# First weights' sums stored unsplit and split where they are used; their making cut into shorter stages; conversion jobs started less densely

## The chip, the cores and the metric

One core of a Trainium2 chip runs the whole program. The metric is the device time of one execution in microseconds (us), lower is better. The engines are TensorE (PE; its weight loads are listed apart as PEld), VectorE (DVE), ScalarE (ACT), GpSimd (POOL), and SyncE (SP), which issues the DMA transfers here. Each engine works through its own instructions in program order and waits for others by semaphores.

## What is computed

Three parts follow each other, in fp32:

```
ret  = (q k^T / 8 * D_h) v                 per batch element b (8) and head h (8), 576 positions
x    = ret, heads side by side             8 x 576 x 512, here 9 blocks of 512 rows
u    = x + (x^T U V)^T                     rank 32 over the positions
x2   = u + max(u w_ch1, 0) w_ch2           512 -> 2048 -> 512
xk, xr = x2 mixed with the row before it   by mu_k, mu_r
out  = sigmoid(xr w_r) * (max(xk w_k, 0)^2 w_v)
```

D_h is a decaying lower triangle. The weights arrive as 64-bit floats.

## The kernel before, in words

All large products run as three fp32r products each: an operand x is kept as a rounded part h (an ACT copy) and a rest l = x - h (a subtraction on DVE or POOL), and h·h, l·h and h·l are added in PSUM.

**The first stage** (about 0 to 496 us) goes through 40 steps, five per batch element. A step does a piece of the retention on PE (`up`, `dn`, with results taken out by DVE as `pm`, `y`, `w`, `xt`), turns an older piece round (`xn`, copied out by ACT as `xs`), and then runs some products of the first weights, `hidden(t, f)`, for an older block t and one of the 16 groups f of 128 columns of w_ch1: 12 matmuls into one of two PSUM banks, left by an ACT ReLU (`hs`, L389) and a store. When a batch element is complete, its eight rank-32 corrections (`mx`, L1028) are placed between the matmuls of `hidden`. They share one PSUM bank with `xn`: the first `mx` waits until ACT has copied `xs`, and each later one waits until DVE has added the one before into `xt` (L1032).

**Conversion jobs** fill the same stage. A job takes 64-bit weights from DRAM to split fp32r values: load, `down` (ACT reads the raw words, L100 and L104), `fill` (DVE joins them, L107), sums (POOL) where the product needs them, `parts` (ACT copies, POOL subtractions) and stores. There are 10 such jobs (`block_weight`) for w_k, w_r and half of w_ch2, and 8 shorter ones for w_v. A list `waiting` holds them. `slot()` takes each job in flight one stage on; whether it also starts a new one is its argument. It is called twice a step while no corrections are due ("quiet" slots, counted in `quiet`).

**Sums of the first weights.** Blocks 7 and 8, the pair, are done in a stage of their own (496 to about 576 us): by Strassen's scheme seven products, m = 1, 7, 5, 2, 6, 4, 3, replace eight, in each of eight groups g (`first_group`, seven times 6 matmuls). This needs four sums of quarters of w_ch1 for each g. `first_sums(g)` makes them in the first stage, one stage of it in each quiet slot: `whole` (4 DVE additions h + l, L298), `sums` (4 DVE operations, L306 to L309), then for each half `part` (ACT copy L314, DVE subtraction L315) and `store` (512 KB). The last store of one g and the `whole` of the next are one stage. `load_first(g)` reads both halves, 1 MB, one group before they are used.

**The way into the pair's stage.** `operands` makes the seven combinations of the pair's rows from `even` (tiles `ue`) and `odd` (a view of the tile `xt` of the last batch element), in small steps set between the last six `hidden` products. `mix_store` has just issued the stores of that `xt` to DRAM (L1055, L1056).

**In the pair's stage** ACT and DVE also take out the products (`f`), and four more conversion jobs (`second_weight`) run at `tick()`.

Of the kernel before, what the change touches and what calls it, by code (L numbers as in the profile page):

```python
# [9 lines left out]
F32 = mybir.dt.float32  # L10
# [33 lines left out]
def retention_mixer_kernel(ctx: ExitStack, tc: tile.TileContext, io):  # L44
# [242 lines left out]
    kept_1 = [dram.tile([128, 2, 2, 2, 256], F32, name=f"first{g}") for g in range(HF)]  # L287

    def first_sums(g):
        got = {}  # L290

        def whole():
            got["x"] = [cv.tile([128, 512], F32, tag="cf", name="cf", bufs=5) for _ in range(2)]
            for i, x in enumerate(got["x"]):
                f = g + HF * i
                w, c = w1[f // 4], slice((f % 4) * 128, (f % 4 + 1) * 128)
                for k in range(2):
                    nc.vector.tensor_tensor(  # L298
                        x[:, 256 * k:256 * k + 256].rearrange("p (k n) -> p k n", n=128),
                        w.h[k][:, :, c].bitcast(F32), w.l[k][:, :, c].bitcast(F32), op=ALU.add,  # L300
                    )

        def sums():
            x, y = got["x"]
            a11, a12, a21, a22 = x[:, :256], x[:, 256:], y[:, :256], y[:, 256:]
            nc.vector.tensor_tensor(a22, a21, a22, op=ALU.add)  # L306
            nc.vector.tensor_tensor(a21, a11, a21, op=ALU.subtract)
            nc.vector.tensor_tensor(a11, a22, a11, op=ALU.subtract)
            nc.vector.tensor_tensor(a12, a12, a11, op=ALU.subtract)  # L309
# [7 lines left out]
        def store(i):  # L317
            nc.sync.dma_start(
                kept_1[g][:, i], got[i].bitcast(F32).rearrange("p l (s n) -> p l s n", n=256)
            )  # L320

        return [whole, sums, lambda: part(0), lambda: store(0), lambda: part(1), lambda: store(1)]

    fs = {}

    def load_first(g):
        for i in range(2):
            x = fs[g, i] = (big2 if g else big).tile([128, 2, 2, 256], F32R, tag="unit", name=f"fw{g}_{i}")
            nc.sync.dma_start(x.bitcast(F32), kept_1[g][:, i])
# [366 lines left out]
    def operands(x, q, a, b, nm, where=None):  # L696
# [18 lines left out]
        less(b[0], b[0], a[0])  # L715
        yield
        lower()
        lower = upper("t1", b[0])
        yield
        less(t, b[1], b[0])  # L720
# [49 lines left out]
    with ExitStack() as st:  # L770
# [412 lines left out]
        for at, job in zip((0, 2, 4, 6, 8, 10, 12, 14, 16, 17), jobs):  # L1183
            waiting.insert(at, job)
# [58 lines left out]

        def step_of(i):
# [31 lines left out]
            for x in range(2):  # L1276
# [24 lines left out]
        while ready:  # L1301
            if len(ready) == 3:
                load_first(0)
# [25 lines left out]
    def first_group(g, base, extra):  # L1329
# [7 lines left out]
        def summed(lo, part, x, i):  # L1337
            return fs[g, part][:, lo, x, col(i)]
# [9 lines left out]
        for m, (b, new, w, nm) in {  # L1348
            1: ("a", True, lambda lo, i: weight(lo, 0, 0, i), "11"),
            7: ("c", True, lambda lo, i: summed(lo, 0, 0, i), "t3"),  # L1350
            5: ("d", True, lambda lo, i: summed(lo, 0, 1, i), "t1"),
# [346 lines left out]
```

## Time and profile before

| | before |
|---|---|
| three runs, median (lowest to highest) | 1390.14 us (1388.85 to 1391.22) |
| the profiled execution: time, span of its instructions | 1390.9 us, 1389.0 us |
| mean granted clock of TensorE | 0.977 |
| PE busy / DVE / ACT / POOL | 97% / 66% / 49% / 27% |
| DMA queue q1 | 343.06 MB, 69.7% of 16 engines |

The profiled execution lies 0.8 us above the median, so what is worked out on it carries over. PE's 97% includes time at half clock: the granted clock is shown as a share of 2.4 GHz, and 0.50 is 1.2 GHz. Rows of a stretch below read: start:end, length, busy us (and number of instructions) of PE, PEld, DVE, ACT, POOL, then the mean granted clock, the mean busy share of the DMA engines, and GB/s. A wait `X <- Y` means that engine X stood idle until Y had finished; its three numbers are us in total, times, and the longest.

### The profile page before, as it was taken

What the parts mean: (1) busy time and instruction counts of PE and PEld (TensorE: products, weight loads), DVE (VectorE), ACT (ScalarE), POOL (GpSimd) and SP (SyncE); (2) the same over time, 40 slices, a digit from 0 to 9 for tenths busy, and PEclk for the clock granted to TensorE, in tenths of its full rate; (3) what the DMA queues carried; (4) which work ended last, traced back from release to release, by engine and by line L of the source; (5) the groups of instructions that cost most, each with busy time, mean ns of one, the idle gap of its engine ahead of it and who ended that gap; (6) DMA issues with size and microseconds to landing.
All of it is one profiled execution on the core that took longest, in us unless ns stands there. A gap on an engine that the chain in (4) does not pass through costs nothing.

```text
span 1389.0 us, 26137 instructions
## 1 busy us (share of the span) xinstructions
PE 1340.4 (97%) x10248; PEld 1099.0 (79%) x10248; DVE 920.1 (66%) x1268; ACT 677.8 (49%) x1185; POOL 380.9 (27%) x317
## 2 busy tenths in 40 slices
PE   6899898999899999999999999999999999999998
PEld 4688787778687787788888888888888888888897
DVE  3634555546353335769888898698687787787753
ACT  4663444446452356644354444465465455465431
POOL 2440344335370013112122222203303303303312
PEclk8899999999999999999999999999999999999999
DMA  9577789989896277999879696888066075074272
GB/s 356 201 246 240 251 312 348 330 314 347 320 346 235 103 241 277 333 409 359 282 243 319 218 309 211 282 285 328 1 244 240 1 275 210 27 277 152 96 279 81
DMA packets 137547, 344.74 MB, mean 248 GB/s; under 512 B 16592, under 2 KB 32336, under 8 KB 137424
## 3 DMA queue, kind: packets, MB, share of 16 engines
q1 hardware_dynamic: 137424, 343.06, 69.7%
q8 instruction: 81, 1.33, 0.4%
q14 instruction: 42, 0.34, 0.1%
HBM read 235.01 MB, written 108.00 MB: 247 GB/s over the span
## 4 chain that ended last, share of the span: by engine, by line
PE 84%; DMA 7%; DVE 5%; ACT 2%; issue 1%; POOL 1%; SPq 0%; DVEq 0%; ACTq 0%; POOLq 0%
PE h L383 19%; PE v L1543 14%; PE gc L557 6%; PE ga L557 6%; PE gd L557 6%; PE kc L1447 4%; PE kd L1447 4%; PE ka L1447 4%; PE gb L557 3%; PE kb L1447 2%; PE rd L1447 2%; PE rc L1447 2%; PE ra L1447 2%; PE xn L977 1%; PE fa L1360 1%
## 5 line engine op out<-in xcount | busy, mean ns | idle before, releaser
L389 ACT ACTIVATE hs<-h 128x512 f32<-128x512 f32 x112 | 66.7, 597 | 177.1 <-PE h L383 173.2
L1499 POOL TENSOR_TENSOR vl<-m,vh 128x512 fp32r<-128x512 f32 (+1 forms) x40 | 47.6, 1191 | 310.2 <-ACT vh L1498 238.9
L516 ACT CAST sbh<-rb 128x1024 fp32r<-128x1024 f32 x64 | 67.3, 1052 | 49.3 <-PE gd L557 41.0
L1543 PE MATMUL v<-vh,wv_0u 128*128 128x512 f32 x288 | 88.8, 389 | 0.0
L1543 PE MATMUL v<-vh,wv_1u 128*128 128x512 f32 x288 | 88.7, 389 | 0.0
L517 DVE TENSOR_TENSOR sbl<-rb,sbh 128x1024 fp32r<-128x1024 f32 x64 | 84.3, 1317 | 3.4 <-ACT sbh L516 3.3
L516 ACT CAST sah<-ra 128x1024 fp32r<-128x1024 f32 (+1 forms) x64 | 53.5, 836 | 57.7 <-DVE ra L498 28.1
L517 DVE TENSOR_TENSOR sal<-ra,sah 128x1024 fp32r<-128x1024 f32 (+1 forms) x64 | 66.5, 1038 | 18.6 <-PE gd L557 10.4
L1032 DVE TENSOR_TENSOR xt<-mx,xt 128x256 f32<-128x256 f32 x64 | 28.8, 457 | 62.1 <-PE mx L1028 62.1
L1499 POOL TENSOR_TENSOR vl<-c,vh 128x512 fp32r<-128x512 f32 (+1 forms) x40 | 62.1, 1573 | 25.9 <-ACT vh L1498 25.9
L1543 PEld LDWEIGHTS v<-vh,wv_1u 128*128 128x128 f32 x288 | 54.1, 188 | 11.2
L1543 PEld LDWEIGHTS v<-vh,wv_0u 128*128 128x128 f32 x288 | 53.9, 188 | 11.1
L801 POOL TENSOR_TENSOR kv<-kv,ktab 128x512 f32<-128x512 f32 (+1 forms) x40 | 40.8, 1019 | 71.6 <-DMA kv<-in_kv 52.9
L1498 ACT CAST vh<-m 128x512 fp32r<-128x512 f32 (+1 forms) x40 | 23.2, 579 | 75.3 <-DVE m L1497 75.3
L315 DVE TENSOR_TENSOR fs<-cf,fs 128x512 fp32r<-128x512 f32 x16 | 13.8, 865 | 67.2 <-ACT fs L314 67.2
L853 DVE TENSOR_TENSOR pm<-up,dtab 128x512 f32<-128x512 f32 (+1 forms) x40 | 25.3, 632 | 48.7 <-PE up L839 48.6
L1543 PE MATMUL v<-vl,wv_0u 128*128 128x512 f32 x144 | 56.0, 389 | 0.0
L1543 PE MATMUL v<-vl,wv_1u 128*128 128x512 f32 x144 | 56.0, 389 | 0.0
L601 POOL TENSOR_TENSOR x<-x,ur 128x512 f32<-128x512 f32 x16 | 25.0, 1574 | 107.5 <-DVE x L597 101.7
L670 ACT ACTIVATE tp<-x2l,omu 128x511 f32<-128x511 f32 x72 | 50.9, 713 | 2.8 <-issue 2.3
L574 POOL TENSOR_TENSOR m<-m,ur 128x512 f32<-128x512 f32 x8 | 12.2, 1550 | 137.2 <-ACT m L571 137.2
L1497 DVE SCALAR_TENSOR_TENSOR m<-m 128x512 f32<-128x512 f32 (+1 forms) x40 | 44.8, 1119 | 1.4
(377 smaller groups left out, 3982.1 us busy)
## 6 DMA issues: line engine op xcount, KB each, us to landing
wk<-keys SPq DMA_DIRECT2D x80, 512.0 KB, 6.0
rb<-hp SPq DMA_DIRECT2D x64, 512.0 KB, 6.4
hp<-hs SPq DMA_DIRECT2D x112, 256.0 KB, 3.9
wr<-gates SPq DMA_DIRECT2D x40, 512.0 KB, 6.7
qk<-in_qk SPq DMA_DIRECT2D x32, 512.0 KB, 6.8
kv<-in_kv SPq DMA_DIRECT2D x32, 512.0 KB, 6.9
ra<-hp SPq DMA_DIRECT2D x32, 512.0 KB, 7.1
ur<-ub SPq DMA_DIRECT2D x18, 512.0 KB, 6.4
```

The source lines that it names most:

```text
L383: nc.tensor.matmul(hps[t, f], w.part(lo, k, fo), u[k // 2][:, k % 2, :], start=(part == 0 and k == 0), stop=(part == 2 and k == KD - 1),)
L389: nc.scalar.activation(h, hps.pop((t, f)), AF.Relu)
L516: nc.scalar.copy(hi_, src)
L517: nc.vector.tensor_tensor(lo_, src, hi_.bitcast(F32), op=ALU.subtract)
L557: nc.tensor.matmul(group[g][p], l[:, col(p)], r, start=(h == 0 and j == 0 and i == 0), stop=(i == 2 and last), skip_group_check=True,)
L670: nc.scalar.activation(tp[:, 1:], x[:, :BT - 1], AF.Copy, scale=omu[:, j, k:k + 1])
L801: nc.gpsimd.tensor_tensor(k, k, ktab[:, p, :n].to_broadcast([128, n, NP, D]), op=ALU.mult)
L1032: nc.vector.tensor_tensor(u, ps[:, :n], u, op=ALU.add)
L1447: nc.tensor.matmul(ps[b], l, r[:, i], start=(part == 0 and i == 0 and j == 0), stop=(i == 1 and j == 2), skip_group_check=True,)
L1497: nc.vector.scalar_tensor_tensor(x, x, 0.0, x, op0=ALU.max, op1=ALU.mult)
L1499: eng.tensor_tensor(l, x, h.bitcast(F32), op=ALU.subtract)
L1543: nc.tensor.matmul(vacc[t][o], w.part(lo, g, col(o)), x[:, i, :], start=(g == 0 and i == 0 and j == 0), stop=(g == NG - 1 and i == 1 and j ...
```

## The change

First weights' sums: `first_sums` now uses one tile of the pool `big` per g instead of two of the small pool `cf`, has five stages (`whole(0)`, `whole(1)`, `sums(0)`, `sums(1)`, `store`) with two DVE operations in each of the first four, makes no split, and stores 512 KB instead of 1 MB. `load_first` reads 512 KB, two groups ahead; `split_first` does one ACT copy and one DVE subtraction of 128x1024 per g, after m = 2 of the group before. `operands` writes one difference over `a[0]` where it wrote over `b[0]`. Conversion jobs start in three of eight quiet slots instead of four, in another order (three jobs of w_k first), and slots go on into the tail of the first stage (`beside`); the last job ends beside `hidden(6, 4)` where it ended beside `hidden(5, 9)`. First sums begin eight slots later.

```diff
-    kept_1 = [dram.tile([128, 2, 2, 2, 256], F32, name=f"first{g}") for g in range(HF)]
+    kept_1 = [dram.tile([128, 4, 256], F32, name=f"first{g}") for g in range(HF)]
...
-        def part(i):
-            x = got["x"][1 - i]
-            y = got[i] = unit(big, F32R, f"fs{g}_{i}")
-            nc.scalar.copy(y[:, 0], x)
-            nc.vector.tensor_tensor(y[:, 1], x, y[:, 0].bitcast(F32), op=ALU.subtract)
...
-        return [whole, sums, lambda: part(0), lambda: store(0), lambda: part(1), lambda: store(1)]
+        def whole(i):
+            if not i:
+                got["x"] = big.tile([128, 4, 256], F32, tag="unit", name=f"fs{g}")
...
+        def store():
+            nc.sync.dma_start(kept_1[g], got["x"])
+
+        return [lambda: whole(0), lambda: whole(1), lambda: sums(0), lambda: sums(1), store]
...
+    def split_first(g):
+        x = fraw.pop(g)
+        fs[g] = h, l = tuple(
+            (big2 if g else big).tile([128, 4, 256], F32R, tag="unit", name=f"f{y}{g}") for y in "hl"
+        )
+        nc.scalar.copy(h, x)
+        nc.vector.tensor_tensor(l, x, h.bitcast(F32), op=ALU.subtract)
...
-        less(b[0], b[0], a[0])
+        less(a[0], b[0], a[0])
         yield
         lower()
-        lower = upper("t1", b[0])
+        lower = upper("t1", a[0])
...
-        for at, job in zip((0, 2, 4, 6, 8, 10, 12, 14, 16, 17), jobs):
+        for at, job in zip((0, 1, 2, 4, 5, 6, 8, 10, 12, 14), jobs):
...
+        def beside():
+            quiet.append(0)
+            slot(new=len(quiet) % 8 in (1, 4, 6))
+            if sums and len(quiet) > 8:
+                sums.pop(0)()
...
-                    quiet.append(i)
-                    slot(new=len(quiet) % 2 == 1 or len(quiet) > 40)
-                    if sums:
-                        sums.pop(0)()
+                    beside()
...
-            hidden(2)
+            hidden(1)
+            beside()
+            hidden(1)
+            beside()
         while todo:
             hidden(1) if ready else mixes(1)
+            beside()
...
-            if len(ready) == 3:
-                load_first(0)
+            if len(ready) in (4, 3):
+                load_first(4 - len(ready))
+            if len(ready) == 1:
+                split_first(0)
...
-            extra[1] = [lambda g=g: load_first(g + 1)]
+            extra[2] = [lambda g=g: split_first(g + 1)]
+        if g + 2 < HF:
+            extra[4] = [lambda g=g: load_first(g + 2)]
```

On DVE, ahead of the first correction (`mx3_0_0`) of block 3: L107 rows are `fill`s of conversion jobs, L298 to L310 make sums of first weights, L853 to L967 are the retention's, L1032 adds the correction. Before:

```order
L107 SCALAR_TENSOR_TENSOR wkf3_3113<-ca_3117,wkf3_3113 128x512
L107 SCALAR_TENSOR_TENSOR cf_3269<-ca_3268,cf_3269 128x512
L306 TENSOR_TENSOR cf_3274<-cf_3274 128x256
L307 TENSOR_TENSOR cf_3274<-cf_3273,cf_3274 128x256
L308 TENSOR_TENSOR cf_3273<-cf_3274,cf_3273 128x256
L309 TENSOR_TENSOR cf_3273<-cf_3273 128x256
L853 TENSOR_TENSOR pm23_3384<-up22_3318,dtab_126 128x512
L950 TENSOR_TENSOR y22_3386<-up22_3318,qtab_127 128x512
L938 TENSOR_TENSOR w4_6_3388<-dn22_3335,w4_5_3202 128x256
L938 TENSOR_TENSOR w4_7_3390<-dn22_3335,w4_6_3388 128x256
L967 TENSOR_TENSOR xt4_3034<-dn22_3335,y22_3386 128x4x128
L1032 TENSOR_TENSOR xt3_2184<-mx3_0_0_3409,xt3_2184 128x256
```

Of the change:

```order
L107 SCALAR_TENSOR_TENSOR wkf3_3050<-ca_3054,wkf3_3050 128x512
L309 TENSOR_TENSOR fs1_2922<-fs1_2922 128x256
L310 TENSOR_TENSOR fs1_2922<-fs1_2922 128x256
L107 SCALAR_TENSOR_TENSOR wrf0_3224<-ca_3225,wrf0_3224 128x512
L298 TENSOR_TENSOR fs2_3261<-w1_0h0_527,w1_0l0_528 128x256
L298 TENSOR_TENSOR fs2_3261<-w1_0h2_626,w1_0l2_627 128x256
L853 TENSOR_TENSOR pm23_3335<-up22_3269,dtab_126 128x512
L950 TENSOR_TENSOR y22_3337<-up22_3269,qtab_127 128x512
L938 TENSOR_TENSOR w4_6_3339<-dn22_3286,w4_5_3164 128x256
L938 TENSOR_TENSOR w4_7_3341<-dn22_3286,w4_6_3339 128x256
L967 TENSOR_TENSOR xt4_2996<-dn22_3286,y22_3337 128x4x128
L1032 TENSOR_TENSOR xt3_2168<-mx3_0_0_3360,xt3_2168 128x256
```

Between two `fill`s and the retention's rows stood a run of four sum operations, and in the slot before it four more (the next L298 rows upwards); now two and two stand there, and the tile they write is one of `big`.

On ACT, from the take-out of `hidden(4, 11)` (`hs4_11`) to the copy `xs6_1`, for which the first correction of block 5 waits (`wsh`, `wv_0p` casts are splits of conversion jobs, L100 and L104 a job's `down`). Before:

```order
L389 ACTIVATE hs4_11_5002<-h4_11_4989 128x512
L270 CAST wsh5_0_5005<-wsf5_4661 128x512 x2
L100 ACTIVATE ca_5012<-wsraw6_0_4835 128x512
L104 ACTIVATE wsf6_5011<-wsraw6_0_4835 128x512
L100 ACTIVATE ca_5015<-wsraw6_1_4837 128x512
L104 ACTIVATE wsf6_5011<-wsraw6_1_4837 128x512
L314 CAST fs6_1_5022<-cf_4671 128x512
L987 COPY xs6_1_5114<-xn6_1_5109 128x512
```

Of the change:

```order
L389 ACTIVATE hs4_11_4907<-h4_11_4894 128x512
L132 CAST wv_0p3_4716<-cf_4593 128x512
L100 ACTIVATE ca_4917<-wsraw6_0_4742 128x512
L104 ACTIVATE wsf6_4916<-wsraw6_0_4742 128x512
L100 ACTIVATE ca_4920<-wsraw6_1_4744 128x512
L104 ACTIVATE wsf6_4916<-wsraw6_1_4744 128x512
L987 COPY xs6_1_5014<-xn6_1_5009 128x512
```

The split of a first weights' sum (`fs6_1`, L314) is gone, and of the jobs' casts one stands there instead of a pair; the `down` has kept its place.

On DVE, the first rows of `operands` (L706 are differences, L703 subtractions that make the l parts). Before:

```order
L706 TENSOR_TENSOR ft_0_6334<-xt7_5591 128x1024
L703 TENSOR_TENSOR fl11_0_6332<-ue0_6040,fh11_0_6331 128x1024
L706 TENSOR_TENSOR xt7_5591<-xt7_5591,ue0_6040 128x2x512
L703 TENSOR_TENSOR flt3_0_6343<-ft_0_6334,fht3_0_6342 128x1024
L706 TENSOR_TENSOR ft_0_6334<-xt7_5591 128x1024
L703 TENSOR_TENSOR flt1_0_6359<-xt7_5591,fht1_0_6358 128x1024
```

Of the change:

```order
L706 TENSOR_TENSOR ft_0_6270<-xt7_5483 128x1024
L703 TENSOR_TENSOR fl11_0_6268<-ue0_5939,fh11_0_6267 128x1024
L706 TENSOR_TENSOR ue0_5939<-xt7_5483,ue0_5939 128x1024
L703 TENSOR_TENSOR flt3_0_6279<-ft_0_6270,fht3_0_6278 128x1024
L706 TENSOR_TENSOR ft_0_6270<-xt7_5483,ue0_5939 128x1024
L703 TENSOR_TENSOR flt1_0_6295<-ue0_5939,fht1_0_6294 128x1024
```

The third row reads the same two tiles and now writes `ue0`, which was read from DRAM, and no longer `xt7`, which is being stored to DRAM; the rows after it read `ue0`.

## Rows read from the trace of the kernel before

**Rows 1.** PE's waits, 110 to 600 us (total us, times, longest us).

```profile
PE mx L1028 <- DVE xt L1032: 10.6, 4, 4.1
PE h L383 <- ACT hs L389: 5.5, 2, 3.4
PE mx L1028 <- ACT xs L987: 4.8, 2, 2.9
```

**Rows 2.** Nine stretches, A to I, each around one stall of PE.

```profile
161.00:174.00 13.00, 9.36 (x62) 7.03 (x55) 4.98 (x10) 3.34 (x7) 1.85 (x2) 0.74 0.60 204
229.00:239.00 10.00, 5.89 (x18) 4.54 (x17) 5.98 (x11) 0.60 (x1) 4.39 (x6) 0.66 1.03 383
273.00:284.00 11.00, 8.90 (x140) 6.83 (x142) 4.97 (x10) 6.72 (x13) 4.15 (x4) 0.84 1.02 395
297.00:308.00 11.00, 7.95 (x30) 6.08 (x29) 6.49 (x13) 0.99 (x3) 2.09 (x3) 0.84 0.92 334
360.00:372.00 12.00, 7.42 (x23) 5.39 (x23) 4.98 (x10) 3.46 (x6) 1.12 (x2) 0.72 1.03 375
418.00:422.00 4.00, 2.41 (x93) 1.99 (x85) 2.64 (x5) 0.00 (x0) 0.26 (x1) 1.00 1.03 320
481.00:492.00 11.00, 7.58 (x23) 5.72 (x22) 9.75 (x9) 6.61 (x8) 0.00 (x0) 0.69 0.26 74
550.00:553.00 3.00, 1.31 (x6) 0.81 (x5) 0.50 (x1) 1.68 (x3) 0.34 (x1) 1.00 0.90 356
579.00:588.00 9.00, 6.92 (x22) 4.64 (x21) 8.56 (x12) 6.96 (x8) 0.00 (x0) 0.81 0.96 325
```

**Rows 3.** DVE's longest wait, 110 to 485 us.

```profile
DVE fs L315 <- ACT fs L314: 67.2, 15, 10.9
```

**Rows 4.** ACT's wait for raw weights, 110 to 485 us.

```profile
ACT ca L100 <- DMA wv_raw<-in_moe_w_v: 9.3, 6, 2.7
```

**Rows 5.** ACT ahead of block 5's mix, timeline (start, us, instruction, idle before).

```profile
357.33 1.13 ACT L270 CAST wsh<-wsf 128x512 fp32r<-128x512 f32 x2
...
360.57 0.66 ACT L104 ACTIVATE wsf<-wsraw 128x512 uint32<-128x512 uint8 x1 [1.52 <-POOL wsl L271]
...
362.36 0.62 ACT L314 CAST fs<-cf 128x512 fp32r<-128x512 f32 x1
362.88 0.58 ACT L987 COPY xs<-xn 128x512 f32<-128x512 f32 x1
```

**Rows 6.** DVE at the same place, timeline.

```profile
363.01 0.69 DVE L315 TENSOR_TENSOR fs<-cf,fs 128x512 fp32r<-128x512 f32 x1 [10.92 <-ACT fs L314]
```

**Rows 7.** One sum line, DVE: ns min/median/max, first and last start.

```profile
L298 DVE TENSOR_TENSOR cf<-w_1h,w_1l x8: 412/1106/1516, 266.5 to 382.9; 128x256 f32<-128x256 f32 x8
```

**Rows 8.** DVE and POOL ahead of block 3's mix, timeline.

```profile
226.97 2.71 POOL L271 TENSOR_TENSOR wkl<-cf,wkh 128x512 fp32r<-128x512 f32 x2 [2.54 <-DMA kv<-in_kv]
227.00 1.54 DVE L307 TENSOR_TENSOR cf<-cf 128x256 f32<-128x256 f32 x1
```

**Rows 9.** The step before the pair's stage, all engines, timeline.

```profile
473.45 1.22 DVE L706 TENSOR_TENSOR ft<-xt 128x1024 f32<-128x1024 f32 x1
...
475.37 1.22 DVE L703 TENSOR_TENSOR fl<-ue,fh 128x1024 fp32r<-128x1024 f32 x1 [0.69 <-ACT fh L702]
...
475.46 0.62 SPq L1056 DMA_DIRECT2D ub<-xt  x1
...
480.10 1.23 DVE L706 TENSOR_TENSOR xt<-xt,ue 128x1024 f32<-128x1024 f32 x1 [3.51 <-DMA ub<-xt]
...
485.35 2.08 PE L383 MATMUL h<-uh,w_3h 128*128 128x512 f32 x4 [3.42 <-ACT hs L389]
```

**Rows 10.** Loads of the pair's split sums, 16 of 512 KB.

```profile
DMA to landing us min/median/max: 4.6/5.5/8.4
```

**Rows 11.** Two long stretches: conversion jobs; the pair's stage.

```profile
180.00:420.00 240.00, 225.53 (x3130) 181.86 (x3129) 126.31 (x210) 118.47 (x226) 113.70 (x104) 0.96 0.95 339
...
496.00:573.00 77.00, 75.31 (x332) 62.03 (x331) 35.98 (x56) 47.14 (x86) 22.57 (x24) 1.00 0.81 276
```

More of the change, by code (lines that the diff above doesn't have):

```diff
@@ L324, in retention_mixer_kernel @@
-    fs = {}
-    def load_first(g):
-        for i in range(2):
-            x = fs[g, i] = (big2 if g else big).tile([128, 2, 2, 256], F32R, tag="unit", name=f"fw{g}_{i}")
-            nc.sync.dma_start(x.bitcast(F32), kept_1[g][:, i])
+        def whole(i):
+            if not i:
+                got["x"] = big.tile([128, 4, 256], F32, tag="unit", name=f"fs{g}")
+            f = g + HF * i
+            w, c = w1[f // 4], slice((f % 4) * 128, (f % 4 + 1) * 128)
+            for k in range(2):
+                nc.vector.tensor_tensor(
+                    got["x"][:, 2 * i + k].rearrange("p (k n) -> p k n", n=128),
+                    w.h[k][:, :, c].bitcast(F32), w.l[k][:, :, c].bitcast(F32), op=ALU.add,
+                )
@@ new lines, in sums @@
+        def sums(i):
+            a11, a12, a21, a22 = (got["x"][:, n] for n in range(4))
+            if not i:
+                nc.vector.tensor_tensor(a22, a21, a22, op=ALU.add)
+                nc.vector.tensor_tensor(a21, a11, a21, op=ALU.subtract)
+            else:
+                nc.vector.tensor_tensor(a11, a22, a11, op=ALU.subtract)
+                nc.vector.tensor_tensor(a12, a12, a11, op=ALU.subtract)
+        def store():
+            nc.sync.dma_start(kept_1[g], got["x"])
+        return [lambda: whole(0), lambda: whole(1), lambda: sums(0), lambda: sums(1), store]
@@ L331, in retention_mixer_kernel @@
+    fs, fraw = {}, {}
+    def load_first(g):
+        fraw[g] = (big if g < 2 else big2).tile([128, 4, 256], F32, tag="unit", name=f"fr{g}")
+        nc.sync.dma_start(fraw[g], kept_1[g])
+    def split_first(g):
+        x = fraw.pop(g)
+        fs[g] = h, l = tuple(
+            (big2 if g else big).tile([128, 4, 256], F32R, tag="unit", name=f"f{y}{g}") for y in "hl"
+        )
+        nc.scalar.copy(h, x)
+        nc.vector.tensor_tensor(l, x, h.bitcast(F32), op=ALU.subtract)
     wkp, wkq = {}, {}
@@ L714, in operands @@
         yield
-        less(b[0], b[0], a[0])
+        less(a[0], b[0], a[0])
         yield
         lower()
-        lower = upper("t1", b[0])
+        lower = upper("t1", a[0])
         yield
-        less(t, b[1], b[0])
+        less(t, b[1], a[0])
         yield
@@ L1335, in weight, with summed @@
             return w1[f // 4].part(lo, 2 * k + i, slice((f % 4) * 128, (f % 4 + 1) * 128))
-        def summed(lo, part, x, i):
-            return fs[g, part][:, lo, x, col(i)]
+        def summed(lo, x, i):
+            return fs[g][lo][:, x, col(i)]
         def out(t, f, x):
@@ L1349, in first_group @@
             1: ("a", True, lambda lo, i: weight(lo, 0, 0, i), "11"),
[L1350 to L1351 removed]
+            7: ("c", True, lambda lo, i: summed(lo, 2, i), "t3"),
+            5: ("d", True, lambda lo, i: summed(lo, 3, i), "t1"),
             2: ("b", True, lambda lo, i: weight(lo, 0, 1, i), "21"),
[L1353 removed]
+            6: ("a", False, lambda lo, i: summed(lo, 0, i), "t2"),
             4: ("c", False, lambda lo, i: weight(lo, 1, 1, i), "t4"),
[L1355 removed]
+            3: ("d", False, lambda lo, i: summed(lo, 1, i), "22"),
         }.items():
```

23 lines of the change are left out of this document (removed).

## The prediction, made before the changed kernel ran

> **What bounds the kernel now.** PE is busy 97% of the span, so I looked first for the time in which it is not, or runs at half clock. The list of PE's waits shows where they lie in the first 600 us: before the rank-32 corrections `mx`, either because DVE has not taken the last one out or because ACT has not copied `xs`, and before `hidden`, because ACT has not taken out `hs` [rows 1]. The reader should see that the sums are small and the single waits long: a few stalls of 2 to 4 us. Then I put a stretch around each stall and read PE's busy time and the granted clock [rows 2]. In A to E, G and I the clock is below 1.00: after such a gap TensorE was granted 1.2 GHz for a while. In F and H, gaps of 1.6 and 1.7 us, it stayed at 2.4. At half clock work takes twice as long, so a stall costs its idle time (length minus PE busy) plus length x (1 - clock):
>
> A 3.64 + 13 x 0.26 = 7.0; B 4.11 + 10 x 0.34 = 7.5; C 2.10 + 11 x 0.16 = 3.9; D 3.05 + 11 x 0.16 = 4.8; E 4.58 + 12 x 0.28 = 7.9; F 1.6; G 3.42 + 11 x 0.31 = 6.8; H 1.7; I 2.08 + 9 x 0.19 = 3.8. Together 45.0 us. A to E lie at the corrections of blocks 2, 3, between, 4 and 5; G is the way into the pair's stage, H lies in that stage, I behind it. Nothing else between 120 and 590 us is to be had, and the change does not reach beyond.
>
> Third, what stands ahead of the late instruction. DVE's longest wait in this stage is L315, the subtraction that splits a first weights' sum, for its ACT copy: 67.2 us in 15 waits, up to 10.9 [rows 3]. ACT is late there because the copy stands behind conversion jobs: at E two casts, the `down` with 1.5 us for POOL, the copy at 362.36, and only then `xs` at 362.88 [rows 5]; DVE stood 10.9 us until 363.01 [rows 6], and pm, y, w, xt and the correction's addition all queue behind it. The `down` of a w_v job waits for its raw words too: 9.3 us in six waits, up to 2.7 [rows 4].
>
> **The change part by part.**
>
> *No split in the first stage.* 16 ACT copies and 16 DVE subtractions of 128x512 go (about 0.62 and 0.69 us each [rows 5, 6]), with all 15 waits of [rows 3]. This takes DVE's part out of A and E. ACT's part: at E, PE waited for `xs` from about 360.6 (the 2.9 us of [rows 1] before 363.5, where `xs` ended). The ACT order of the change has one cast (0.6) and four `down` rows (four times 0.6) between `hs4_11` and `xs6_1`. Counted from `hs4_11`'s end, some 357.4, just ahead of the first cast, that gives `xs` at about 361.0, or 362.5 with POOL's 1.5 us: 0.4 to 1.9 us late, and no clock lost where a gap of 1.7 lost none. I take E at 1 and A, whose `xs` loses a copy, a cast and a wait for raw words, at 0.
>
> *Shorter stages.* At B, C and D the run of eight sum operations stands ahead of the retention's rows. One of them takes 0.41 us alone but 1.1 in the median of one line and up to 1.5 [rows 7]; at B one of 1.54 lies inside two POOL subtractions of 2.71 [rows 8]. Eight at 0.42 are 3.4 us, at 1.1 they are 8.8; the stalls' idle parts are 2.1 to 4.1. With two and two per slot the run is 0.8 to 2.2 us, and no slot holds a fourth piece. I take B, C and D at 0: B's two `fill`s and four sums now stand where ten operations stood. Bounds: 0 and 16.2, all three as they are.
>
> A rule speaks against this. The Trainium skill ("SBUF — State Buffer", Who interferes with whom) says that a DVE instruction with two SBUF inputs shares a read interface with a GpSimd instruction that reads SBUF, and that the second of them blocks until the first is done. The rows agree in kind, 1.54 against 0.41. The 64 two-input sums are as many after as before, so by this rule their sum of waiting stays and only its length in one place changes.
>
> *Jobs spread wider.* The 18 jobs stand in new slots, 50 for 44, and the last ones in a stretch where DMA has room. That the same casts, `down`s and POOL subtractions fall ahead of other corrections is the unknown: ahead of block 4's first correction there is now a w_v `down`, which may wait 2.7 us for its words [rows 4]. Also the sums now write a tile of `big`, and DVE waits for its last user; for the fifth sum that is a job's split that is stored one slot earlier. Lower bound 0, upper bound all of A to E, 31.1. Between them I allow two new stalls of D's size, 9.6 us: two of the five block boundaries have such a job ahead.
>
> *`operands` writes `ue`.* G: DVE stood 3.51 us for the store of `xt`, because it wrote over what was being read; the difference started at 480.10 although its inputs were there at 476.6 [rows 9]. From 476.6, with 1.22 per operation, the three up to the second next difference end at 480.2; ACT's copy (two of 0.62 at most) and `hs` (0.6) follow at 482.1, against 481.9 when PE began to wait (485.35 - 3.42). So the first gap is 0.2. The next `hs` stands behind three more DVE operations (483.9), a copy and itself: 485.7, while PE has done its next twelve matmuls (0.227 each, 75.31 / 332 [rows 11]) at 484.8: 0.9. G falls from 6.8 to 1.1 and saves 5.7, at the least the 3.5 of the wait.
>
> *Split in the pair's stage.* Eight ACT copies of at most 1.24 and eight DVE subtractions of 1.22 are added to 47.1 and 36.0 us busy of 77 [rows 11]: 57.0 and 45.8. PE is busy throughout, a product is 1.36 us, a group 9.5. A load is issued after m = 4 and its split stands after m = 2 of the next group, 5 products or 6.8 us later; loads landed in 4.6 to 8.4 [rows 10], so ACT may stand for 1.6. Behind it are the copy of m = 6 and ReLUs; the next thing that PE needs from ACT is product 1's copy of the next group, before product 6, seven products or 9.5 us on, in which ACT has about 57.0 / 8 = 7.1 of work. 2.4 us are spare: cost 0. H has its own cause, raw words of another job, and stays; so does I, though 4 MB less are loaded.
>
> **Sum.** -7.0 (A) -7.5 (B) -3.9 (C) -4.8 (D) -6.9 (E) -5.7 (G) + 9.6 = -26.2. From the profiled 1390.9 that is 1364.7, and 0.8 less for the median: 1364.
>
> **The rivals.**
>
> - *Nearly all gone.* No new stalls, and I and H shrink with the fewer loads by 2: 1390 - 35.8 - 2 = 1352. For it: all waits of [rows 3] are gone. Against: the jobs are still there.
> - *The transfers are the bound.* From 180 to 420 us the DMA engines are busy 0.95 at 339 GB/s [rows 11]. If they set the pace, only bytes count: eight stores of 512 KB less are 4.2 MB, 12.4 us at that rate, and G: 1390 - 12.4 - 5.7 = 1372. For it: loads would land later in a shorter stage. Against: at B and C 383 and 395 GB/s were moved [rows 2], and PE's waits end on DVE and ACT.
> - *POOL holds up the sums as before.* Each sum still meets POOL's subtractions, as the one of 1.54 us did [rows 8], and the delay reaches the corrections: C, D and half of B, 12.4 us, stay: 1376. This is what the Trainium skill's rule on the shared interface would make of the change. For it: the median of 1.1 in [rows 7]; against it: the run ahead of a correction is half of what it was or less.
> - *The jobs' new places give all back*: 31 us of new stalls beyond G and E; within 0.2%, 1390.
> - *Slower: raw sums arrive late in the pair's stage.* It decides at a landing of 6.8 + 2.4 = 9.2 us. At 13, six groups (g = 2 to 7) would each lose 3.8 and, like C, 1.8 of clock: 34 us, so that 1364 becomes 1398. For it: DMA is at 0.81 there. Against: fewer bytes, and 8.4 was the longest.
>
> **How the numbers follow.** Forecast (1357 to 1369) 0.42, nearly all gone 0.13, transfers 0.17, POOL 0.13, all given back 0.06, slower 0.09. A measurement of this kernel tells 0.2%, 2.8 us, from no change: faster 0.85, same 0.06, slower 0.09. The range of 8 in 10 goes from just below the second case to above the fourth, with some of new stalls on top: 1351 to 1381.
>
> **What would show it.** PE's wait for DVE's corrections, 10.6 us, should fall below 3, that for `hs` below 2; DVE should have no wait of over 5 us for ACT but at `fill`s; the granted clock should be 1.00 from 470 us on and the mean near 0.985. In the pair's stage PE should be as busy as before. The prediction is wrong if PE waits before corrections as long as before, behind `down`, `fill` or `big`, or if waits for `f` or the new splits appear in every group.

## The result, and the profile after

The changed kernel takes 1371.81 us (median of 4 runs, 1370.29 to 1373.39), the kernel before, in the same session, 1389.49 (1387.03 to 1391.22). The ratio is 0.9874, with a 95% interval of 0.9852 to 0.9896: 17.7 us faster, where 26 were forecast. The profiled execution took 1373.39 us with a span of 1371.3, and its mean granted clock was 0.986.

The page of the changed kernel, part 1 and the rows for TensorE's clock and the DMA engines in 40 slices:

```profile
span 1371.3 us, 26089 instructions
...
PE 1332.1 (97%) x10248; PEld 1090.8 (80%) x10248; DVE 921.3 (67%) x1260; ACT 677.5 (49%) x1177; POOL 382.8 (28%) x317
...
PEclk8799999999999999999999999999999999999999
DMA  9676789889886566999788796787085075174271
```

PE's waits from 110 to 600 us after the change, which answer to [rows 1] (total us, times, longest us):

```profile
PE mx L1028 <- ACT xs L987: 7.0, 2, 6.9
PE fc L1369 <- DVE fl L329: 3.1, 4, 0.8
PE gall L998 <- issue: 2.2, 1, 2.2
PE ga L557 <- ACT sah L516: 1.2, 1, 1.2
PE h L383 <- issue: 0.8, 1, 0.8
PE fc L1369 <- ACT fh L328: 0.8, 2, 0.4
PE mx L1028 <- DVE xt L1032: 0.8, 1, 0.8
PE h L383 <- ACT hs L389: 0.7, 2, 0.5
```

The wait for DVE's corrections went from 10.6 us to 0.8, that for `hs` from 5.5 to 0.7. What stands at the head is new: one wait of 6.9 us for `xs`, and six waits in the pair's stage, 3.9 us in all, for the split that was moved there.

DVE's and ACT's waits from 110 to 485 us, those that answer to [rows 3, 4] or are new:

```profile
DVE cf L107 <- ACT cf L104: 18.1, 5, 9.7
DVE fs L298 <- DMA gates<-wrl: 8.4, 1, 8.4
...
ACT ca L100 <- DMA wv_raw<-in_moe_w_v: 17.8, 4, 8.3
```

L315's 67.2 us are gone with the line. Two waits for transfers have grown in their place: ACT's for raw words from 9.3 us (longest 2.7) to 17.8 (longest 8.3), and VectorE's for the store of a job's halves, 8.4 us at once.

Stretches after the change, which answer to [rows 2, 11] (us; busy us of PE, PEld, DVE, ACT, POOL; clock, DMA share, GB/s):

```profile
222.00:232.00 10.00, 9.14 (x42) 7.14 (x42) 5.51 (x12) 1.33 (x3) 0.61 (x1) 1.00 1.02 367
281.00:293.00 12.00, 5.11 (x18) 3.90 (x18) 5.31 (x12) 1.91 (x4) 3.74 (x5) 0.72 1.05 380
400.00:409.00 9.00, 6.77 (x99) 5.48 (x89) 3.55 (x7) 1.66 (x4) 5.18 (x7) 0.81 0.74 251
467.00:478.00 11.00, 10.51 (x47) 8.34 (x46) 5.50 (x5) 5.86 (x9) 0.00 (x0) 1.00 0.65 202
475.00:552.00 77.00, 72.42 (x309) 57.12 (x308) 42.48 (x60) 51.02 (x88) 23.99 (x24) 1.00 0.63 205
563.00:572.00 9.00, 7.15 (x29) 5.00 (x28) 8.23 (x10) 6.97 (x8) 0.00 (x0) 1.00 0.98 333
180.00:420.00 240.00, 228.87 (x3175) 185.39 (x3174) 124.27 (x218) 109.19 (x207) 104.14 (x97) 0.98 0.89 315
```

The same arithmetic as in the prediction (length minus PE busy, plus length times one minus the clock) makes the stretch at 281 us cost 6.89 + 12 x 0.28 = 10.3 us, more than any one of A to I; the one at 400 us (F's place) costs 2.23 + 9 x 0.19 = 3.9. G's place lost only 0.5 us. In the pair's stage PE was busy for 72.42 of 77 us, against 75.31 [rows 11].

How the 17.7 us came about, by the time at which the last instruction of each step ended in the two traces (the last `hs` of a block, the first and last product of the pair's stage, the last product of the items behind it):

| up to | before, us | after, us | change in this step |
|---|---|---|---|
| end of block 1 | 181.66 | 174.55 | -7.1 |
| end of block 2 | 247.24 | 235.83 | -4.3 |
| end of block 3 | 314.20 | 302.55 | -0.2 |
| end of block 4 | 380.51 | 361.84 | -7.0 |
| end of block 5 | 442.67 | 426.62 | +2.6 |
| pair's stage begins | 496.24 | 474.92 | -5.3 |
| pair's stage ends | 574.58 | 558.61 | +5.4 |
| items end | 885.67 | 868.11 | -1.6 |
| end | 1389.00 | 1371.28 | -0.2 |

Blocks 1, 2 and 4 and the way into the pair's stage won 23.7 us. Three places took from it: block 3, where a new stall ate C's and D's gain, block 5, where F's place went from 1.6 to 3.9 us, and the pair's stage. The 1.6 us of the items' step need not be the change's: before, the clock stood at 1.2 GHz for 3.4 us at the items' start, and of the fourteen traces of this study seven show that and seven do not.

**The stall in block 3.** Timeline at 275 to 289 us, ACT, DVE, SP's queue and PE (start, us, instruction, idle before and what ended it):

```profile
279.68 0.35 SPq L184 DMA_DIRECT2D wv_raw<-in_moe_w_v  x1
...
280.28 0.77 DVE L298 TENSOR_TENSOR fs<-w_1h,w_1l 128x256 f32<-128x256 f32 x2 [8.43 <-DMA gates<-wrl]
...
287.08 0.66 ACT L100 ACTIVATE ca<-wv_raw 128x512 f32<-128x512 f32 x1 [8.33 <-DMA wv_raw<-in_moe_w_v]
...
288.19 0.58 ACT L987 COPY xs<-xn 128x512 f32<-128x512 f32 x1
...
288.91 0.55 PE L1028 MATMUL mx<-vst,gt 96*128 96x256 f32 x1 [6.89 <-ACT xs L987]
```

SP issued the load of a w_v job's raw words only at 279.68, behind other transfers; it landed 7.4 us later. ACT came to the `down` (L100) at 278.7, stood there 8.33 us, and `xs`, for which the mix waits, stood behind it. From 271.9 to 280.3 VectorE waited to write the fifth sum's tile until the gates' halves in it had been stored. One trace gives the size of such a stall to some 3 us only: in e4 and e13 below, whose edits lie behind this stage, the gap is 6.38 and 5.29 us, with 6.83 and 3.41 us at half clock behind it, against 6.89 and 6.83 here.

**The pair's stage.** Timeline at 499 to 506 us:

```profile
502.64 0.64 ACT L104 ACTIVATE w2f<-w2raw 128x512 uint32<-128x512 uint8 x1
...
503.70 1.03 ACT L328 CAST fh<-fr 128x1024 fp32r<-128x1024 f32 x1
504.77 1.23 DVE L329 TENSOR_TENSOR fl<-fr,fh 128x1024 fp32r<-128x1024 f32 x1 [2.65 <-ACT fh L328]
...
506.05 0.50 PE L1369 MATMUL fc<-fht,fl 128*128 128x512 f32 x1 [0.77 <-DVE fl L329]
```

The raw sums are there long before (the load of them, L321, landed in 3.6 to 4.8 us). But ACT, busy with the words of a `second_weight` job, reaches the split's copy 4.3 us after the last matmul of product m = 2 (499.4), and product 7 of the next group, which reads the halves, has to wait.

### The profile page after: what moved, and what is told of

It is laid out like the page before. It is cut to its first block, busy times and chain, and to the rows that moved or that the text cites. A ratio compares the mean times of both kernels' runs of the same rounds, so it can differ in the third digit from the quotient of the medians.

```text
span 1371.3 us, 26089 instructions
## 1 busy us (share of the span) xinstructions
PE 1332.1 (97%) x10248; PEld 1090.8 (80%) x10248; DVE 921.3 (67%) x1260; ACT 677.5 (49%) x1177; POOL 382.8 (28%) x317
## 4 chain that ended last, share of the span: by engine, by line
PE 56%; DVE 2%; issue 1%; DMA 1%; ACT 0%; DVEq 0%; ACTq 0%
PE v L1554 14%; PE gc L557 6%; PE ga L557 6%; PE gd L557 6%; PE ka L1458 3%; PE kd L1458 3%; PE kc L1458 3%; PE gb L557 3%; PE kb L1458 2%; PE rd L1458 2%; PE rc L1458 2%; PE ra L1458 2%; PE c L639 1%; PE c L637 1%; PE c L638 1%; PE rb L1458 1%
## 5 line engine op out<-in xcount | busy, mean ns | idle before, releaser
L853 DVE TENSOR_TENSOR pm<-up,dtab 128x512 f32<-128x512 f32 (+1 forms) x40 | 25.4, 634 | 91.3 <-PE up L839 91.3
L1032 DVE TENSOR_TENSOR xt<-mx,xt 128x256 f32<-128x256 f32 x64 | 28.8, 457 | 51.6 <-PE mx L1028 51.6
L1458 PE MATMUL kc<-kht,wk 128*128 128x512 f32 (+1 forms) x160 | 45.5, 368 | 0.0
```

The source lines that it names most:

```text
L853: nc.vector.tensor_tensor(m[:, :, :n], t[:, :, 0:n * 128].rearrange("p g (x i) -> p g x i", i=2 * L), dtab.to_broadcast([128, 2, n, 2 * L] ...
L1032: nc.vector.tensor_tensor(u, ps[:, :n], u, op=ALU.add)
L1458: nc.tensor.matmul(ps[b], l, r[:, i], start=(part == 0 and i == 0 and j == 0), stop=(i == 1 and j == 2), skip_group_check=True,)
```

## The experiments

Each is compared with the kernel before, run on the same chip beside it; where two experiments are compared, the ratios count more than the medians, since the kernel before itself took 1385.3 to 1389.5 us on the chips used.

**e1: only the operands write `ue`** (the rest as before):

```
-        less(b[0], b[0], a[0])
+        less(a[0], b[0], a[0])
...
-        less(t, b[1], b[0])
+        less(t, b[1], a[0])
```

> The kernel before with nothing but the edit of operands (the difference is written over a[0], the tile ue, not over b[0], the tile xt that is being stored). Theory: DVE's 3.5 us wait for the store is all there is to the stall on the way into the pair's stage, so the gap of 3.4 us and 3.4 us of half clock go but for a residual of about 1: 5.7 us faster, about 1384. Rival: the wait only moves to the next DVE operation or to ACT's copies, and PE's gap stays at 2 us or more: under 3 us faster. The stalls before the corrections and the pair's stage stay as they are in either case.

Measured 1381.09 us, ratio 0.9940 (0.9922 to 0.9959) to 1388.72: 7.6 us. PE's wait for `hs` at this place fell to 0.5 us.

**e2: the change without that edit** (the lines above the other way round):

> The changed kernel with the edit of operands taken back. Theory: the stall of the kernel before comes back whole at the last hidden products, 6 to 7 us against the 0.5 us gap there now: about 1377 to 1378. Rival: the conversion jobs and sums that ended elsewhere had made ACT and DVE late there, and without them the wait is covered: within 2 us of the changed kernel.

Measured 1378.11 us, ratio 0.9928 (0.9900 to 0.9955), 6.3 us over the changed kernel. PE's waits from 460 to 490 us:

```profile
PE h L383 <- ACT hs L389: 3.4, 1, 3.4
```

The 3.42 us of [rows 9] are back to the hundredth, at 467.41 us. From both sides this edit is worth 6 to 8 us: the forecast's 5.7 was small, since it is G nearly whole.

**e3: the raw words one slot earlier:**

```
-        return [load, down, fill, None, None, split] + ([after] if after else [])
+        return [load, None, down, fill, None, split] + ([after] if after else [])
```

> The changed kernel with one empty stage between load and down of the eight jobs of w_v, so that their raw words have two slots to land instead of one. Theory: the 6.9 us gap before the correction of block 4 (and 3.4 us at half clock) is ACT standing 8.3 us for raw words that were issued late and landed late, so it goes and nothing takes its place: 8 to 10 us faster than the changed kernel, about 1362. Rival: DVE, which stood 8.4 us in the same slot for the store of a job's split in a tile that a sum is to be written to, was as late as ACT: the gap stays, with DVE as its releaser, and less than 4 us are won.

Measured 1368.62 us, ratio 0.9859 (0.9834 to 0.9883). ACT's wait for `wv_raw` is gone, but 6.7 of the stall's 10.3 us stay (3.26 us, and 6.83 at half clock). Its timeline there, DVE and PE:

```profile
278.30 0.76 DVE L298 TENSOR_TENSOR fs<-w_1h,w_1l 128x256 f32<-128x256 f32 x2 [8.55 <-DMA gates<-wrl]
...
284.29 0.63 PE L1028 MATMUL mx<-vst,gt 96*128 96x320 f32 x1 [3.26 <-DVE xt L1032]
```

VectorE's wait for the gates' store had been hidden behind ACT's: the rival held. The stall had two causes, and the profile of the changed kernel names only the one that ended last. The intervals of the two ratios, here and of the changed kernel, overlap.

**e4: the split earlier in its group** (the load too, from m = 4 to m = 2):

```
-            extra[2] = [lambda g=g: split_first(g + 1)]
+            extra[1] = [lambda g=g: split_first(g + 1)]
```

> The changed kernel with the split of a group's sums after m = 1 of the group before instead of after m = 2, and its load after m = 2 instead of m = 4. Theory: in the pair's stage ACT is 3 to 4 us late where a conversion job's words or casts stand ahead of the split, so copy and subtraction miss product 7 of the next group; three products more (4.1 us) cover that, and the stage falls from 83.7 us to 78 or less: 5 us faster, about 1366.5. Rival: ACT and DVE have too much work in the stage as a whole; then the gaps move to waits for f or for another copy and less than 2 us are won.

Measured 1375.38 us, ratio 0.9901 (0.9870 to 0.9932). The stage took 83.7 us as without the edit; only what PE waits for has changed. Its waits for ACT in the stage:

```profile
PE fa L1369 <- ACT f L1375: 2.7, 2, 2.5
PE fc L1369 <- ACT f L1375: 2.5, 2, 2.0
```

My theory that the split's place was at fault fell. At either place ACT is late with something that PE needs from it: there the halves, here the copy of a product.

**e5: the sums' stages in one** (two stages where the change has four):

```
-        return [lambda: whole(0), lambda: whole(1), lambda: sums(0), lambda: sums(1), store]
+        return [lambda: (whole(0), whole(1)), None, lambda: (sums(0), sums(1)), None, store]
```

> The changed kernel, with the sums' stages put back to one whole stage (four additions) and one of four operations, with an empty stage behind each. Theory (short stages matter): one stage then holds VectorE for 2.4 to 3.5 us instead of 1.2 to 1.7, and block corrections and the keys' corrections that come due meanwhile start up to 1.7 us later; new waits of TensorE for VectorE of 1 to 2 us each in three or four blocks, with half clock behind the longer ones, 1376 to 1382 us. Rival (most of the stalls before came from the split parts and their ScalarE copies, not from the stages' length): the time stays within 3 us of the changed kernel, 1369 to 1375.

Measured 1373.27 us, ratio 0.9890 (0.9875 to 0.9905), whose interval overlaps that of the change. No new wait for VectorE appeared, so two stages in place of four cost at most a few us: the rival held. What the prediction credited at B and C is not tested by this, though. Counted in DVE's timelines from 110 to 500 us, eight sum operations stood between two pieces of the retention three times in the kernel before (from 121, 222 and 267 us; at D, from 295 us, there were four), and never more than four in the changed kernel, nor in e5. No run puts a run of eight back.

**e6: the jobs at their old places:**

```
-        for at, job in zip((0, 1, 2, 4, 5, 6, 8, 10, 12, 14), jobs):
+        for at, job in zip((0, 2, 4, 6, 8, 10, 12, 14, 16, 17), jobs):
...
-            slot(new=len(quiet) % 8 in (1, 4, 6))
+            slot(new=len(quiet) % 2 == 1 or len(quiet) > 40)
```

> The changed kernel, with the conversion jobs at the places that they had before and started as before (every second quiet step). Theory (spreading the jobs gave a part): the pair's stage then begins 3 to 8 us later, since ScalarE's conversions bunch up again beside the sums, 1375 to 1380 us, and the stall of 6.89 us in the fourth block goes away or moves since the gates' job no longer stands right ahead of the fifth sum. Rival (the places give nothing by themselves, and the stall of the fourth block is theirs): 1364 to 1370, the stall gone and nothing put in its place.

Measured 1374.83 us, ratio 0.9901 (0.9886 to 0.9915). The large stall is gone, and smaller ones came (3.5, 2.8, 1.5 and 1.0 us). PE's waits from 110 to 600 us:

```profile
PE h L383 <- ACT hs L389: 4.0, 2, 3.5
PE mx L1028 <- ACT xs L987: 3.6, 2, 2.8
...
PE mx L1028 <- DVE xt L1032: 2.5, 2, 1.5
```

The 2.8 us are at E's place: block 4 took 63.6 us, against 59.3 with the new places and 66.3 before. So it is neither theory nor rival in full: the new places brought the one long stall and took away others of much the same sum; the pair's stage begins only 0.4 us later (475.3), so the spreading has not relieved ACT by the 3 to 8 us that I expected. The 3 us between the medians lie at the edge of what the intervals tell apart.

**e7: the bytes as before** (each sum stored a second time, to a tile that nobody reads):

```
             nc.sync.dma_start(kept_1[g], got["x"])
+            nc.sync.dma_start(spare_1[g], got["x"])
```

> The changed kernel, with each sum stored a second time, to a spare tile in DRAM that nobody reads: the stores of the sums carry as many bytes as before the change again (8 times 512 KB more, 4.2 MB). Rival of the prediction (transfers bound the stretch from 180 to 420 us, so that the change won by its halved bytes): 4.2 MB at the 339 GB/s of [rows 11] are 12 us, and the time goes to 1381 to 1385 us. Theory (single waits bound it, and the transfers lie beside TensorE's work): within 3 us of the changed kernel, 1369 to 1375; the share of the DMA engines rises in that stretch and TensorE's busy time stays.

Measured 1381.82 us, ratio 0.9954 (0.9939 to 0.9969): 10.0 us over the changed kernel, near the rival's price and far from the theory's. This was the surprise of the study. Its waits from 110 to 600 us:

```profile
ACT ca L100 <- DMA wv_raw<-in_moe_w_v: 21.8, 4, 8.6
PE mx L1030 <- ACT xs L989: 10.4, 4, 7.8
DVE fs L299 <- DMA gates<-wrl: 9.8, 1, 9.8
```

The long stretch, by its window:

```profile
180.00:420.00 240.00, 225.82 (x3092) 182.45 (x3095) 120.70 (x212) 106.21 (x202) 103.75 (x97) 0.96 0.92 329
```

TensorE does not run slower throughout, as it would if transfers set its pace. It loses the time in four gaps (2.24, 1.66, 7.83 and 1.24 us) and at half clock behind two of them, and the longest, 6.89 in the changed kernel, ends on ACT's `xs`, behind 8.6 us for raw words. By the steps of the table block 2 took 65.4 us, as long as before the change (65.6), where the change had brought 61.3. Two things limit this run: the two profiled executions lie only 5.6 us apart, so the traces show no more than that of the 10, and the edit also gives SP eight more transfers to issue, which no run tells from the bytes.

**e9: the sums in a tile of their own**, on top of e3 (one buffer, since there was room for one when `big` gave up one of its 35):

```
-                got["x"] = big.tile([128, 4, 256], F32, tag="unit", name=f"fs{g}")
+                got["x"] = cv.tile([128, 4, 256], F32, tag="fs", name=f"fs{g}", bufs=1)
```

> The raw words are loaded one slot earlier, as in e3_raw_one_slot_earlier, and besides the sums have a tile of their own (one buffer; the big pool has one buffer fewer), so that a sum's first addition waits for no store of a job's halves. Theory (the fourth block's stall had two causes, ScalarE waiting for the raw words and VectorE waiting for the tile of the gates' halves): the 3.26 us that were left at 281 us and the 6.83 us of half clock behind them go, 1361 to 1364 us. Rival (something else is late behind both, or the buffer that is missed in the big pool makes a new wait): the gap stays above 1 us or moves, 1366 to 1370.

Measured 1409.37 us, ratio 1.0158 (1.0132 to 1.0185): 21 us slower than the kernel before, and outside both expectations. DVE's longest wait from 110 to 485 us:

```profile
DVE fs L298 <- DMA first<-fs: 88.6, 7, 18.2
```

The timeline where it is longest:

```profile
210.34 0.76 DVE L298 TENSOR_TENSOR fs<-w_0h,w_0l 128x256 f32<-128x256 f32 x2 [18.24 <-DMA first<-fs]
...
214.30 2.08 PE L383 MATMUL h<-uh,w_2h 128*128 128x512 f32 x4 [10.31 <-ACT hs L389]
```

The code puts the last stage of a sum (its store) and the first addition of the next into one step. With one buffer that addition waits seven times for the store issued in the same step, up to 18.2 us (here SP came to the store at 203.99, 12 us after DVE had begun to wait, and it landed 6.3 us later), and the retention's work queues behind it. The edit put a worse wait where it meant to remove one, so it says nothing on the theory.

**e12: VectorE makes both halves in the pair's stage**, on top of e9:

```
-        nc.scalar.copy(h, x)
+        (nc.vector.tensor_copy if g else nc.scalar.copy)(h, x)
```

> As e9_sums_tile_apart, and in the pair's stage the high half of the raw sums is copied by VectorE instead of ScalarE (from the second group on). Theory (the split is late because ScalarE, full of second_weight's words, comes to the copy 4 us after the second product, while VectorE is free): VectorE's low half is done by 504.6 us of the changed kernel's time instead of 505.9, TensorE's waits for L329 and L328 go, and the pair's stage takes 78 to 81 us instead of 83.7; 3 to 5 us less than e9_sums_tile_apart, 1357 to 1360. Rival (VectorE gets as late as ScalarE, since it waits for ScalarE's copies of the products anyway): the stage stays within 1.5 us of 83.7 and the time within 1.5 us of e9_sums_tile_apart.

Measured 1402.11 us, ratio 1.0106 (1.0082 to 1.0131), 7.3 us less than without it, where 3 to 5 were expected; the pair's stage went from 83.7 to 77.5 us. **e13: the same edit on the changed kernel alone:**

> The changed kernel with one edit: in the pair's stage VectorE makes the high half of the raw sums too (from the second group on). Theory (ScalarE's lateness at this copy is the whole of what the split costs in the pair's stage): the stage goes from 83.7 to 77.5 us, as it did from e9_sums_tile_apart to e12_split_copy_on_vector, and nothing changes ahead of it: 1364 to 1367 us. Rival (the gain there came with that kernel's other state of the buffers): the stage stays above 81 us, 1369 or more.

Measured 1365.76 us, ratio 0.9837 (0.9821 to 0.9853), and again 77.5 us for the stage: the theory held. DVE's timeline in the place shown above:

```profile
497.63 0.68 DVE L1381 TENSOR_TENSOR f<-fb,f 128x512 f32<-128x512 f32 x1
498.23 0.68 DVE L328 CAST fh<-fr 128x1024 fp32r<-128x1024 f32 x1
498.95 1.23 DVE L329 TENSOR_TENSOR fl<-fr,fh 128x1024 fp32r<-128x1024 f32 x1
```

The first 77 us of the stage, by their window:

```profile
471.00:548.00 77.00, 76.60 (x336) 62.44 (x335) 52.38 (x71) 48.29 (x86) 25.28 (x24) 1.00 0.65 226
```

VectorE goes on to the split at once, since nothing of the job's words stands ahead of it. DVE is busier than in [rows 11] by 16 us in 77 and PE does not wait for it: for VectorE it was not how much work it had that counted, but what stood ahead of the instruction. For ACT this is not separated: the edit takes 1.03 us a group off it together with the place in its order, and e4, which changed the place alone, won nothing. The stage itself is steady: 83.7 us in all eight traces with the raw sums and ACT's copy, 77.5 or 77.6 in all four with VectorE's.

**e15, three cures**: e3, e13, and the fifth sum's first addition in a step of its own:

```
-            if sums:
+            if sums and g != 4:
                 before, begin = sums[-1], x[0]
                 sums[-1] = lambda before=before, begin=begin: (before(), begin())
```

> The changed kernel with the raw words loaded one slot earlier (e3), VectorE's copy in the pair's stage (e13), and the fifth sum's first addition in a step of its own instead of in that of the fourth sum's store, so that it comes one step later, when the gates' halves whose tile it writes have been stored. Theory (this wait is what e3 left at 281 us, 3.26 us and 6.83 us of half clock): the gap falls below 1 us and the clock stays whole there; 1355 to 1358 us. Rival (the tile comes no sooner, or the step that the later sums are moved by makes a new wait): the time is that of e3 less the pair's stage's 6, 1361 to 1364.

Measured 1359.61 us (1356.28 to 1362.29), ratio 0.9793 (0.9771 to 0.9815) to 1387.80: the fastest of all, 28 us under the kernel before. PE's waits over 0.6 us from 110 to 600 us:

```profile
PE mx L1028 <- DVE xt L1032: 2.0, 2, 1.2
PE ga L557 <- ACT sah L516: 1.2, 1, 1.2
PE mx L1028 <- ACT xs L987: 0.7, 1, 0.7
```

The stretch of the stall and the long one:

```profile
281.00:293.00 12.00, 10.81 (x50) 8.57 (x49) 6.17 (x14) 2.80 (x6) 3.41 (x5) 1.00 1.04 385
...
180.00:420.00 240.00, 236.98 (x3262) 191.94 (x3261) 132.98 (x223) 115.10 (x217) 109.22 (x100) 1.00 0.92 328
```

The gap is 1.19 us with a whole clock, but the second wait is not gone. DVE and PE in its timeline:

```profile
279.95 0.76 DVE L298 TENSOR_TENSOR fs<-w_1h,w_1l 128x256 f32<-128x256 f32 x2 [8.13 <-POOL wv_0p L133]
...
283.68 0.41 PE L1028 MATMUL mx<-vst,gt 96*128 96x320 f32 x1 [1.19 <-DVE xt L1032]
```

The profile names POOL, whose instruction ended at 279.79; the last store of the gates' halves landed at 279.78. So VectorE stood nearly as long as in e3 (8.55), until 1.3 us before the first correction's product, there 1.5. What the edit changed is the work behind that wait: in e3 a `fill` and the sum's second pair of additions came before the retention's rows, here they do not, and from the start of L298 to the correction's addition it is 3.26 us in place of 5.52. That is the 2.1 us by which the gap shrank. My theory, that the tile would be free in time, did not hold, and the rival was right on the tile but not on the time. The profiled execution was the fastest of its four; the median lies 1.6 us above the theory's bound. The row of the long stretch matters for e7: with the DMA engines busy 0.92, as much as there, TensorE works 237 of 240 us.

**e16: the bytes as before, on e15:**

> e15_three_cures with every sum stored a second time to a spare tile, as in e7_bytes_as_before. There the 4.2 MB cost 10 us, and TensorE lost them in single gaps (2.24 and 7.83 us for ScalarE's xs, 1.66 us for VectorE, and 17.1 us at half clock in their wake). Theory (the bytes cost by making the raw words of the conversion jobs land later than the engines that wait for them can bear, not because transfers bound the whole stretch): with the words loaded a slot earlier there is slack for this, and the time stays within 4 us of e15, 1358 to 1364 us. Rival (transfers bound the stretch, so bytes cost time whatever is cured): 8 to 12 us again, 1368 to 1372.

Measured 1364.85 us, ratio 0.9851 (0.9828 to 0.9874) to 1385.29. The medians differ by 5.2 us, the ratios by 0.0058, which is 8 us. Either is above the theory's 4, and the ratio is in the rival's range; the intervals of the two ratios leave about 4 to 12 us. Its timeline ahead of block 3's mix and in block 3:

```profile
222.37 0.35 PE L1031 MATMUL mx<-vst,gt 96*128 96x256 f32 x1 [1.97 <-ACT xs L990]
...
286.50 0.76 DVE L300 TENSOR_TENSOR fs<-w_1h,w_1l 128x256 f32<-128x256 f32 x2 [9.83 <-DMA gates<-wrl]
```

VectorE's wait for the gates' store, 8.13 us in e15, is 9.83 here, and a gap of 2.82 us follows from it; two more (1.97 and 2.03 us) stand at block 3's first corrections. So my theory, that one slot of slack would take up the bytes, is not borne out: they cost time with the cures too. By which transfers is only in part seen. Over all transfers issued from 180 to 420 us the median landing was 5.9 us, against 5.6 in e15; the last of the gates' stores landed 5.0 us after its issue in both, but was issued 1.7 us later, counted from when VectorE began to wait.

## Why the prediction was right in sign and too high in gain

- **A (7.0) and E (6.9)** were right in number: block 1 gave 7.1 and block 4 gave 7.0. A went with the split, or with the sums' later start, which no run separates from it: with the operands, the stages, the places or the bytes put back, block 1 still takes 58.4 to 59.5 us, against 64.9 before. E hung on the jobs' places as well: e6 has no split in this stage either, and 4.3 of the 7.0 us came back there.
- **B (7.5)** gave 4.3. At its place PE now loses 0.9 of 10 us at whole clock, so the stall is gone; another gap of 0.8 us is part of the rest, and what else the block lost I have not located. With the bytes put back it took 65.4 us in e7 and in e16, against 65.6 before, so what it gave needs the saved bytes.
- **C and D (8.7)** went, and in the same block the new stall of 10.3 us came. Whether the shorter runs of sums did it is not shown, since e5 has no run of eight; at D four stood in a row before as well, so there the prediction read the order wrongly.
- **G (5.7)** gave 5.3 in the trace, and 6.3 to 7.6 by the medians of the two runs that isolate it. Right.
- **The allowance for new stalls (9.6)** was mis-sized in its terms. Its place was named, the w_v job's `down` and the `big` tile ahead of block 4's first correction, but the step took the longest wait for raw words of before, 2.7 us [rows 4], for what the new slot would bring. In the profiled execution it measured 8.3, the tile's wait 8.4, and the stall 10.3 with its half clock; F's place went from 1.6 to 3.9 besides. Together 10.3 + 2.3 = 12.6, against 9.6. The landings would have told more: in the trace of before these loads took 5.8 us in the median and up to 6.8 from issue to landing, which is what an engine waits that comes to the words right after the issue.
- **The split in the pair's stage (0)** is the step that failed: it costs 5.4 us, and e13, with the copy on VectorE, gives 6 back. The prediction counted how long ACT may stand for the load, and what is queued behind the split. It didn't count the split's own deadline. From m = 2 to product 7 of the next group are four products of 1.36 us, 5.4; the two operations take 1.03 + 1.23; so ACT may come to it 3.2 us late, and with a `second_weight` job's words ahead of it it came 4.3 late. An average of 7.1 us of work in 9.5 says nothing of that. Nor was this deadline all: in e4 the halves were in time, and ACT's lateness met the products' copies instead, for the same 83.7 us.
- **H and I** were to stay: H's place shows 0.6 us in place of 1.7, and the step that holds I gave 1.6, which by the other traces is chance.

Of the rivals, late raw sums did not happen (landings of 3.6 to 4.8 us), nor did nearly all go, nor was all given back. *POOL holds up the sums* can't be the cause of the time that was missing: e15 has the same 64 sums, with means up to 1.17 us (L298), and hardly a gap left. The Trainium skill ("SBUF — State Buffer", Who interferes with whom) says that a two-input VectorE operation contends with a GpSimd instruction that reads SBUF; 1.17 against 0.41 us alone agrees with that, but little of it still reaches PE, whose waits for corrections in e15 are 2.0 us in all.

*The transfers are the bound* gave 1372 and the time is 1371.8, which is partly chance: that sum holds neither the stall nor the split. But it saw something that the forecast dismissed. Putting back the 4.2 MB costs 10 us (e7), so the saved bytes are a large part of the gain. The argument against it was that PE's waits end on DVE and ACT. They do, and yet DVE and ACT were waiting for a landing. What it had wrong is the pace: a stretch with as busy DMA engines runs nearly without gaps in e15.

Added up one at a time, the bytes (10.0), the operands (6.3), the jobs' places (3.0) and the stages (1.5), less the split (6.1 by e13), make 14.7 of the 17.7 us by the medians; by the ratios the same sum is about 19. The missing split's own ACT and DVE time and the sums' later start were not run alone, and the parts need not add.

The signs that the prediction set were met in the first stage: waits for corrections 0.8 and `hs` 0.7, no wait of DVE over 5 us for ACT but at `fill`s, mean clock 0.986 and 1.00 in the stretches from 467 us on. The last one, PE as busy in the pair's stage as before, failed, and that was the term.

## What to carry to other kernels

A step that is moved has two slacks: what waits behind it, and its own deadline counted from the last moment at which its engine can come to it, with the longest run of foreign work ahead of it and not the mean. DMA engines at 0.9 need not set the pace, and added bytes can cost time all the same (e7, e16), so for each wait on ACT or DVE ask whether that engine was itself waiting for a transfer. Where a stall has two causes, the profile names the one that ended last; curing it shows the other (e3). A wait can also go on under another name (e15), so its length and its end are to be compared, not only the name; and where it stays, less work between it and what PE needs still helps.

## What the runs showed of the hardware

- The same copy of 128x1024 f32 to fp32r took 1.03 us on ACT and 0.68 on VectorE, where the subtraction of the same size takes 1.23. The Trainium skill ("VectorE: DVE Perf Modes", Mode 2×_2P — use both read ports for one tensor) says that one-source fp32 operations in SBUF go twice as fast as two-source ones; the row agrees, 0.68 to 1.23.
- A gap's length alone did not decide whether the clock fell. Two gaps of 1.23 and 0.53 us (to 0.01) stand at the items' start in every trace; they were followed by 3.4 us at 1.2 GHz in seven of them (the kernel before, e1, e4, e5, e6, e7 and e16) and by none in the other seven, the changed kernel's among them. A single gap of 2.82 us in e16 left the clock at 2.4 GHz (1.00 from 284 to 299 us), one of 2.23 us in the changed kernel did not (0.81 in the stretch at 400 us). What tells them apart is open.
